# Cosformer attention and SwiGLU on one core: features of q turned whole, early loads uncast, banks by age

## The chip, the cores and the metric

The kernel runs on one core of a Trainium2 chip. The metric is device time in microseconds (us), the median of several executions. "Span" is the profiled execution's own length, some 2 us shorter than its time. "Turned" means transposed, "uncast" loaded without a change of type. TensorE multiplies, VectorE and ScalarE do elementwise work, GpSimd issues the loads that cast (the software queue), SP issues uncast loads, stores and DMA transposes (the hardware queue). The profile counts the packets of both queues on the same 16 DMA engines. Batches are numbered 0 to 7.

## The reference, cut to what matters

```python
# q, k, v: (8 batches, 8 heads, 576 positions, 64), float32
theta = np.pi / 2.0 * pos / S
phi = lambda x: np.concatenate([relu(x) * cos(theta), relu(x) * sin(theta)], axis=-1)
kv  = einsum('bhsf,bhsd->bhfd', phi(k), v)         # 128 features x 64
num = einsum('bhsf,bhfd->bhsd', phi(q), kv)
den = einsum('bhsf,bhf->bhs',  phi(q), sum of phi(k) over s) + 1e-06
x   = (num / den), heads side by side              # 4608 tokens x 512
out = (silu(x @ w_gate) * (x @ w_val)) @ w_out     # d_ff = 1536
```

## The kernel before

The 4608 tokens are nine groups of 512; a group is four tiles of 128 tokens, and a tile is two slots of 64 tokens. A group's FFN has 12 steps of 8 products and then 4 output tiles of 12 products. Attention for the next group is planned into numbered places between those steps: group g has places 16g to 16g + 15. In these traces TensorE runs its products in program order: while one waits, those behind it wait too.

For batches 2 to 7, q passes a ReLU on ScalarE, is turned by a DMA transpose, and each tile makes four products of 260 columns. They hold the cosine and the sine part apart; ScalarE and VectorE weight and add them afterwards:

```python
def qturn_dma(b, e):
    nc.sync.dma_start_transpose(out=qt_of(b)[:, e]..., in_=st[b, "q"][e * SH:(e + 1) * SH]...)

def a_half(t, j):                      # twice for each tile
    ps = take(2)
    for e in range(2):
        nc.tensor.matmul(out=ps[ms, e, 0:4 * D1], lhsT=st[b, "qt"][:, e, j, c:c + n]...,
                         rhs=kvd[b % 2][:, e, j]..., start=True, stop=True)   # 260 columns
    nc.scalar.activation(out=tmp, in_=av[:, :, 0], func=AF.Copy, scale=cst[:, c0, 0:1])
    nc.vector.scalar_tensor_tensor(out=num, in0=av[:, :, 1], scalar=cst[:, c0, 1:2], in1=tmp, ...)
```

Of the kernel before, what the change touches and what calls it, by code (L numbers as in the profile page):

```python
# [17 lines left out]
def kernel(  # L18
# [26 lines left out]
    R = 2 * T  # L45
# [3 lines left out]
    rel = ctx.enter_context(tc.tile_pool(name="rel", bufs=2))  # L49
    qtp = ctx.enter_context(tc.tile_pool(name="qtp", bufs=2))  # L50
    kvp = ctx.enter_context(tc.tile_pool(name="kvp", bufs=2))
# [11 lines left out]
    bank_at = [0]  # L63
    held = {}

    def take(n, hold=None):

        while True:
            b0 = (bank_at[0] + n - 1) // n * n % 8
            bank_at[0] = b0 + n  # L70
            if not any(b0 <= x < b0 + n for r in held.values() for x in r):
                break
        if hold is not None:
            held[hold] = range(b0, b0 + n)
        return banks[:, b0] if n == 1 else banks[:, b0:b0 + n]

# [23 lines left out]
    first = {}  # L100
    CUT = (4, 5)

    def load_first(nm, gs, cs=slice(0, NC)):
        if nm not in first:
            first[nm] = consts.tile([P, G, cs.stop, D], FP32, name=f"first_{nm}")
        nc.sync.dma_start(out=first[nm][:, gs, cs].rearrange("p g c d -> p g (c d)"),
                          in_=source(0, nm)[:, gs, cs.start * D:cs.stop * D])

    pairs = (slice(0, 2), slice(2, 4))
    for gs in pairs:  # L110
        load_first("v", gs)
    load_first("q", slice(0, G), slice(0, CUT[0]))
    pos_i = consts.tile([P, NC], mybir.dt.int32)
    nc.gpsimd.iota(pos_i, pattern=[[1, NC]], base=0, channel_multiplier=NC)
# [3 lines left out]
    for j in range(2):  # L118
        t = consts.tile([P, 8 * J * D1], BF16, name=f"kvd_{j}")
        nc.gpsimd.memset(t.bitcast(FP32), 0.0)  # L120
        kvd.append(t.rearrange("p (e j w i x) -> p e j w i x", e=2, j=J, w=2, i=2))
    load(0, "k", 2)
    load_slots(0, "q", CUT[0], NC)

# [4 lines left out]
    def idle_products(n):  # L129
        ps = take(1)  # L130
        for _ in range(n):
            nc.tensor.matmul(out=ps, lhsT=zeros, rhs=zeros.unsqueeze(1).to_broadcast([P, 4, P]), start=True, stop=True)  # L132

    idle_products(28)


    rad = math.pi / 2.0 / S
    bias = consts.tile([P, 3, 2], FP32)
    pos = consts.tile([P, NC], FP32)
    for i, step in enumerate((S, S - 1, S + NC - 1)):  # L140
        for e in range(2):
            hs = slice(e * SH, (e + 1) * SH)
            nc.vector.memset(bias[hs, i, 0:1], math.pi / 2.0 + e * rad * step)
            nc.vector.memset(bias[hs, i, 1:2], -e * rad * step)
        if i == 0:
            nc.vector.tensor_copy(out=pos, in_=pos_i)
    csk = consts.tile([P, NC, 2], FP32)
    cst = consts.tile([P, NC, 2], FP32)
    last = slice(NC - 1, NC)
    for i, cs, sl in ((0, csk, slice(0, NC)), (1, cst, slice(0, NC - 1)), (2, cst, last)):  # L150
        nc.scalar.activation(out=cs[:, sl, 0], in_=pos[:, sl], func=AF.Sin, scale=-rad, bias=bias[:, i, 0:1])
        nc.scalar.activation(out=cs[:, sl, 1], in_=pos[:, sl], func=AF.Sin, scale=rad, bias=bias[:, i, 1:2])
    tiny = consts.tile([P, 1], FP32)
    nc.scalar.activation(out=tiny, in_=bias[:, 0, 0:1], func=AF.Silu)
# [14 lines left out]
    wo_sb = consts.tile([P, FC, d_model], BF16)  # L169
# [26 lines left out]
    def relu_q(b, g):  # L196
        if g == 0:
            st[b, "q"] = rel.tile([P, J, NC, 2, D], BF16, name="r_q")
        relu_op("act", st[b, "q"][:, g // 2, :, g % 2], raws[b, "q"][:, g])

    def vmul(b, g):
        nc.vector.tensor_tensor(  # L202
            out=v2s[b % 2][:, g, :, :, 0:D],
            in0=(first if b == 0 and g < 2 else {"v": raw_of(b, "v")})["v"][:, g].unsqueeze(2).to_broadcast([P, NC, 2, D]),
            in1=tab, op=ALU.mult,
        )

    def qt_of(b):
        if (b, "qt") not in st:
            st[b, "qt"] = qtp.tile([P, 2, J, NC, SH], BF16, name="qt")  # L210
        return st[b, "qt"]

    def qturn_dma(b, e):
        nc.sync.dma_start_transpose(
            out=qt_of(b)[:, e].rearrange("p j c s -> p (j c) s"),
            in_=st[b, "q"][e * SH:(e + 1) * SH].rearrange("p j c i d -> p (j c i d)"),
        )
# [34 lines left out]

    def kv_free(b):
        held.pop(("kv", b))


    NW = 8
    qw = consts.tile([P, 2, J, NW, 2, D], BF16)
    qwT = {}

    def weight_q(c, w, eng):
        o, sc = qw[:, w, :, c], csk[:, c, w:w + 1]
        i = (first["q"] if c < CUT[0] else raw_of(0, "q"))[:, :, c].rearrange("p (j i) d -> p j i d", i=2)
        if eng == "act":
            nc.scalar.activation(out=o, in_=i, func=AF.Relu, scale=sc)
        else:
            nc.vector.tensor_scalar(out=o, in0=i, scalar1=sc, scalar2=0.0, op0=ALU.mult, op1=ALU.max)

    def turn_qw(t):
        qwT[t] = consts.tile([P, 2, 2, J, 2, SH], BF16, name=f"qwT_{t % 2}")  # L270
        for w, eng in enumerate(("act", "dve")):
            ps = take(1).bitcast(BF16).rearrange("p (y e s) -> p y e s", e=2, s=SH)
            for j in range(J):
                for c in range(2):
                    nc.tensor.transpose(out=ps[:, 2 * j + c].rearrange("p e s -> p (e s)"),
                                        in_=qw[:, w, j, 2 * t + c].rearrange("p i d -> p (i d)"), identity=ident)
            (nc.scalar.copy if eng == "act" else nc.vector.tensor_copy)(  # L277
                out=qwT[t][:, w].rearrange("p e j c s -> p (j c) e s"), in_=ps[:, 0:2 * J])

    def a_tile(t):  # L280
        ps = take(2)
        for e in range(2):
            for j in range(J):
                for w in range(2):
                    nc.tensor.matmul(  # L285
                        out=ps[:, e, 2 * j * D1:2 * (j + 1) * D1],
                        lhsT=qwT[t][:, w, e, j].rearrange("p c s -> p (c s)"),
                        rhs=kvd[0][:, e, j, w].rearrange("p i x -> p (i x)"),
                        start=(w == 0), stop=(w == 1),
                    )  # L290
        num = ps[:, :, 0:2 * J * D1].rearrange("p e (y x) -> p e y x", x=D1)
# [4 lines left out]
        nc.vector.reciprocal(out=rec, in_=den)  # L296
        x = xp.tile([P, d_model], BF16, name="x")
        nc.vector.tensor_tensor(
            out=x.rearrange("p (y e d) -> p e y d", e=2, d=D), in0=num[:, :, :, 0:D],
            in1=rec.rearrange("p (e y) o -> p e y o", e=2).to_broadcast([P, 2, 2 * J, D]), op=ALU.mult,  # L300
        )
# [46 lines left out]
    def x_turn(t, fast=False):  # L348
        x = st.pop(("x", t))
        tg, off = divmod(t, GH // 2)  # L350
        if tg not in xT:
            xT[tg] = xtp.tile([P, KC, T], BF16, name="xT")
        o = xT[tg][:, :, off * P:(off + 1) * P]
        if fast:
# [7 lines left out]

    ht = consts.tile([P, FC, R], BF16, name="ht")

    def ffn_mm(tg, fc, lo=0, hi=GH):

        n = (hi - lo) * SH
        ts = slice(lo * SH, hi * SH)
# [6 lines left out]
        for o, w in zip(ps, (wg_sb, wv_sb)):  # L375
            for kc in range(KC):
                nc.tensor.matmul(out=o, lhsT=w[:, kc, fs], rhs=xT[tg][:, kc, ts],  # L377
                                 start=(kc == 0), stop=(kc == KC - 1))
        st["f", tg, fc, lo] = ps

    def ffn_act(tg, fc, lo=0, hi=GH):
# [4 lines left out]
        r = (tg * T + lo * SH) % R  # L386
        nc.vector.tensor_tensor(out=ht[:, fc, r:r + n], in0=sg[:, 0:n], in1=ps[1], op=ALU.mult)  # L387
# [8 lines left out]
    def ffn_out(t, f0=0, f1=None):  # L396
# [4 lines left out]
        r = (t * P) % R  # L401
        for fc in range(f0, f1):
            nc.tensor.matmul(out=o_ps[t], lhsT=ht[:, fc, r:r + P], rhs=wo_sb[:, fc],  # L403
# [4 lines left out]
        held.pop(("o", t))  # L408
# [6 lines left out]
    def ffn_out_last(t):  # L415

        r = (t * P) % R
        for lo, hi in ((0, 320), (320, d_model)):
            ps = take(1)[:, 0:hi - lo]
            for fc in range(FC):  # L420
                nc.tensor.matmul(out=ps, lhsT=ht[:, fc, r:r + P], rhs=wo_sb[:, fc, lo:hi],  # L421
# [9 lines left out]
    for i in range(4):  # L431
        load_w(i)
# [32 lines left out]


    vmul(0, 0)
    vmul(0, 1)
    for g in (2, 3):
        nc.scalar.copy(out=raw_of(0, "v")[:, g], in_=first["v"][:, g])  # L470
        vmul(0, g)
    for c in range(CUT[0]):
        weight_q(c, 0, "act")
        weight_q(c, 1, "dve")
    relu_k(0, 0, 2, "dve")
    turn_qw(0)
    kv_mm(0, 0)
    idle_products(2)
    relu_k(0, 2, 4, "dve")
    turn_qw(1)  # L480
    kv_out(0, js=slice(0, 1))
    kv_mm(0, 1)
    idle_products(4)
    kv_out(0, js=slice(1, 2))
    kv_free(0)
    a_tile(0)
    a_tile(1)
    idle_products(3)
    for c in (4, 5):
        weight_q(c, 0, "act")  # L490
        weight_q(c, 1, "act")
    x_turn(0, fast=True)
    turn_qw(2)
    for c in (6, 7):
        weight_q(c, 0, "act")
        weight_q(c, 1, "dve")
    a_tile(2)
    for f in range(2):
        ffn_fc(0, f, 0, 2)
    x_turn(1, fast=True)  # L500
    turn_qw(3)
    for f in range(2):
        ffn_fc(0, f, 2, 4)
    x_turn(2, fast=True)
    a_tile(3)
# [108 lines left out]
```

## Time and profile before

| | before |
|---|---|
| time, median | 339.96 us (339.66 to 344.24); 339.81 with a fourth execution |
| span of the profiled run | 337.0 us, TensorE clock 1.00 |
| first FFN product | 18.23 us |
| group 1 starts | 61.55 us |
| a group in steady state | 34.36 or 34.82 us |

The prediction below shows the views that it rests on. One line that it passed over is from the view of the turned q tile: the times of its twelve DMA transposes from issue to landing.

```profile
DMA to landing us min/median/max: 3.7/3.9/10.2
```

### The profile page before, as it was taken

What the parts mean: (1) busy time and instruction counts of PE and PEld (TensorE: products, weight loads), DVE (VectorE), ACT (ScalarE), POOL (GpSimd) and SP (SyncE); (2) the same over time, 40 slices, a digit from 0 to 9 for tenths busy, and PEclk for the clock granted to TensorE, in tenths of its full rate; (3) what the DMA queues carried; (4) which work ended last, traced back from release to release, by engine and by line L of the source; (5) the groups of instructions that cost most, each with busy time, mean ns of one, the idle gap of its engine ahead of it and who ended that gap; (6) DMA issues with size and microseconds to landing.
All of it is one profiled execution on the core that took longest, in us unless ns stands there. A gap on an engine that the chain in (4) does not pass through costs nothing.

```text
span 337.0 us, 5960 instructions
## 1 busy us (share of the span) xinstructions
PE 325.9 (97%) x2280; PEld 167.6 (50%) x2313; DVE 189.0 (56%) x424; ACT 158.0 (47%) x311; POOL 32.4 (10%) x50
## 2 busy tenths in 40 slices
PE   8889998999999999999999999999999999999995
PEld 3578854454444444444454444544454444444443
DVE  6664756389526952695259625971478138714420
ACT  6664456778326732673257415751354135413321
POOL 9454320011002000200000000000000000000000
PEclk9999999999999999999999999999999999999999
DMA  8999999999976828492810271017301410141013
GB/s 238 198 200 200 204 207 208 252 185 186 159 150 100 147 58 168 72 168 48 160 27 17 48 153 45 16 31 143 71 17 31 104 38 16 34 109 31 0 33 93
DMA packets 57084, 36.76 MB, mean 109 GB/s; under 512 B 31328, under 2 KB 52064, under 8 KB 57056
## 3 DMA queue, kind: packets, MB, share of 16 engines
q0 software_dynamic: 20624, 18.03, 33.8%
q1 hardware_dynamic: 36272, 18.23, 25.9%
q8 instruction: 18, 0.29, 0.3%
q10 hardware_dynamic: 160, 0.13, 0.1%
q14 instruction: 10, 0.08, 0.1%
HBM read 37.75 MB, written 9.44 MB: 140 GB/s over the span
## 4 chain that ended last, share of the span: by engine, by line
PE 93%; ACT 3%; DVE 2%; issue 1%; ACTq 0%
PE banks L377 53%; PE banks L403 27%; PE banks L316 5%; PE banks L132 3%; PE banks L237 3%; ACT sg L385 1%; DVE v L202 1%; DVE ht L387 1%; PE banks L357 1%; PE banks L421 0%; PE banks L285 0%; ACT xT L358 0%; PE banks L223 0%; ACT ob L410 0%; ACT qwT L277 0%
## 5 line engine op out<-in xcount | busy, mean ns | idle before, releaser
L377 PE MATMUL banks<-xT,wg_sb 128*128 128x512 bf16 (+2 forms) x474 | 112.4, 354 | 1.8 <-ACT xT L358 1.0
L387 DVE TENSOR_TENSOR ht<-sg,banks 128x512 bf16<-128x512 bf16 (+2 forms) x122 | 76.1, 624 | 66.4 <-PE banks L377 50.9
L377 PE MATMUL banks<-xT,wv_sb 128*128 128x512 bf16 (+2 forms) x479 | 111.7, 354 | 0.2
L385 ACT ACTIVATE sg<-banks 128x512 bf16<-128x512 f32 (+2 forms) x122 | 66.9, 548 | 90.3 <-PE banks L377 89.4
L403 PE MATMUL banks<-wo_sb,ht 128*128 128x512 bf16 x410 | 93.3, 379 | 0.6 <-issue 0.2
L377 PEld LDWEIGHTS <-wv_sb 128*128 128x128 bf16 x488 | 47.3, 98 | 46.3
L377 PEld LDWEIGHTS <-wg_sb 128*128 128x128 bf16 x488 | 45.8, 98 | 37.1 <-issue 2.2
L403 PEld LDWEIGHTS <-ht 128*128 128x128 bf16 x420 | 40.7, 98 | 46.1 <-issue 0.6
L410 DVE COPY ob<-banks 128x512 f32<-128x512 f32 x17 | 11.8, 692 | 56.3 <-PE banks L403 56.2
L326 ACT ACTIVATE tmp<-banks,cst 128x260 f32<-128x260 f32 x64 | 30.5, 477 | 13.6 <-PE banks L316 12.8
L410 ACT COPY ob<-banks 128x512 f32<-128x512 f32 x18 | 10.6, 587 | 55.9 <-PE banks L403 55.9
L327 DVE SCALAR_TENSOR_TENSOR num<-banks,cst,tmp 128x260 f32<-128x260 f32 x64 | 31.0, 485 | 7.1 <-ACT tmp L326 6.7
L316 PE MATMUL banks<-kvd,qt 128*128 128x260 bf16 (+1 forms) x144 | 24.9, 277 | 0.1
L341 DVE TENSOR_TENSOR x<-num,rec 128x256 bf16<-128x256 f32 x64 | 24.4, 422 | 1.1
L202 DVE TENSOR_TENSOR v<-raw_v,tab 128x1152 bf16<-128x1152 bf16 x30 | 22.3, 752 | 0.0
L316 PEld LDWEIGHTS <-qt 128*128 128x128 bf16 (+1 forms) x144 | 11.8, 100 | 16.0 <-issue 3.4
L188 ACT ACTIVATE raw_k<-raw_k 128x576 bf16<-128x576 bf16 x24 | 16.0, 675 | 0.0
L188 ACT ACTIVATE r_q<-raw_q 128x576 bf16<-128x576 bf16 x24 | 16.0, 675 | 0.0
L93 POOL DMA_DIRECT2D raw_k<-in_k_dram x9 | 7.0, 780 | 82.1 <-issue 78.9
L237 PE MATMUL banks<-v,raw_k 64*64 64x130 bf16 x576 | 11.9, 220 | 1.1 <-ACT kvd L249 0.9
L237 PEld LDWEIGHTS <-raw_k 64*64 64x64 bf16 x576 | 9.2, 106 | 7.0 <-issue 5.6
L132 PE MATMUL banks<-zeros 128*128 128x512 bf16 x37 | 11.1, 458 | 1.0 <-DVE zeros L127 1.0
(57 smaller groups left out, 113.0 us busy)
## 6 DMA issues: line engine op xcount, KB each, us to landing
out_dram<-ob SPq DMA_DIRECT2D x70, 128.0 KB, 2.4
raw_k<-in_k_dram POOLq DMA_DIRECT2D x7, 576.0 KB, 12.5
raw_v<-in_v_dram POOLq DMA_DIRECT2D x6, 576.0 KB, 13.6
raw_q<-in_q_dram POOLq DMA_DIRECT2D x6, 576.0 KB, 15.6
wg_sb<-in_moe_w_gate_dram POOLq DMA_DIRECT2D x6, 256.0 KB, 11.3
wv_sb<-in_moe_w_val_dram POOLq DMA_DIRECT2D x6, 256.0 KB, 11.3
wo_sb<-in_moe_w_out_dram POOLq DMA_DIRECT2D x3, 512.0 KB, 13.3
first_v<-in_v_dram SPq DMA_DIRECT2D x2, 576.0 KB, 4.2
```

What stands on the lines that cost most here:

```text
L188: nc.scalar.activation(out=out, in_=in_, func=AF.Relu)
L202: nc.vector.tensor_tensor(out=v2s[b % 2][:, g, :, :, 0:D], in0=(first if b == 0 and g < 2 else {"v": raw_of(b, "v")})["v"][:, g].unsqueeze ...
L237: nc.tensor.matmul(out=ps[i * D:(i + 1) * D, e, j * 2 * D1:(j + 1) * 2 * D1], lhsT=raws[b, "k"][es, g, c], rhs=v2s[b % 2][es, g, c, :, 0:D ...
L316: nc.tensor.matmul(out=ps[ms, e, 0:4 * D1], lhsT=st[b, "qt"][:, e, j, c:c + n].rearrange("p c s -> p (c s)"), rhs=kvd[b % 2][:, e, j].rear ...
L326: nc.scalar.activation(out=tmp, in_=av[:, :, 0], func=AF.Copy, scale=cst[:, c0, 0:1])
L327: nc.vector.scalar_tensor_tensor(out=st["num", t][:, j], in0=av[:, :, 1], scalar=cst[:, c0, 1:2], in1=tmp, op0=ALU.mult, op1=ALU.add,)
L341: nc.vector.tensor_tensor(out=x[:, 4 * j * D:(4 * j + 4) * D].rearrange("p (i e d) -> p e i d", i=2, e=2), in0=num[:, hs, 0:D].rearrange(" ...
L377: nc.tensor.matmul(out=o, lhsT=w[:, kc, fs], rhs=xT[tg][:, kc, ts], start=(kc == 0), stop=(kc == KC - 1))
L385: nc.scalar.activation(out=sg[:, 0:n], in_=ps[0], func=AF.Silu)
L387: nc.vector.tensor_tensor(out=ht[:, fc, r:r + n], in0=sg[:, 0:n], in1=ps[1], op=ALU.mult)
L403: nc.tensor.matmul(out=o_ps[t], lhsT=ht[:, fc, r:r + P], rhs=wo_sb[:, fc], start=(fc == 0), stop=(fc == FC - 1))
L410: (nc.scalar.copy if t % 2 == 0 else nc.vector.tensor_copy)(out=ob, in_=ps)
```

## The change

It has three intents. The start is to be earlier: k, v and the first q come uncast through SP, and weights are held behind v. PSUM banks (the eight pieces of memory that TensorE writes its products to) are taken by age instead of in rotation. From batch 2 on, q is multiplied by cosine and sine before it is turned, so that one product of 65 columns per head is complete and the weighting after it goes. The turned q is then twice as large. Tile 9 is used three places later than before, and x of tiles 9 to 11 is turned on TensorE instead of by DMA. The core of the diff, cut:

```diff
-        relu_op("act", st[b, "q"][:, g // 2, :, g % 2], raws[b, "q"][:, g])
+        relu_op("act", o, o)
+        nc.vector.tensor_tensor(out=st[b, "q"][:, g], in0=o.unsqueeze(2).to_broadcast([P, NC, 2, D]),
+                                in1=tab, op=ALU.mult)
...
         nc.sync.dma_start_transpose(
-            out=qt_of(b)[:, e].rearrange("p j c s -> p (j c) s"),
+            out=phit[b][:, e].rearrange("p g c s -> p (g c) s"),      # twice as many columns
...
+    def a_tile2(t):
...
+        for e in range(2):
+            for g in range(G):
+                for ms, b, c, n in parts:
+                    nc.tensor.matmul(out=ps[ms, e, g * D1:(g + 1) * D1],
+                        lhsT=phit[b][:, e, g, c:c + n].rearrange("p c s -> p (c s)"),
+                        rhs=kv2s[b % 2][:, e, g // 2, g % 2], start=True, stop=True)
+        x_of(t, ps)
...
+    b0 = min(free, key=lambda b: sorted(used[b:b + n], reverse=True))
...
+    nc.gpsimd.tensor_copy(out=hold, in_=first["v"][:, 1, 0, 0:1])    # weights wait for v
+    load_w(0)
+    load_slots(0, "q", CUT[0], NC)
...
+        elif tg == 2:                                                # tiles 9 to 11
+            at((10, 11, 12)[i - 1] + SLOTS, lambda t=t: a_tile2(t))
+            at((12, 13, 14)[i - 1] + SLOTS, turn(t, True))
```

## The prediction

> **What bounds the kernel now.** I read the page's totals first, then busy time by stretch (cut at the first product of each group of 512 tokens), then TensorE's instructions in order of time.
>
> ```profile
> PE 325.9 (97%) x2280; PEld 167.6 (50%) x2313; DVE 189.0 (56%) x424; ACT 158.0 (47%) x311; POOL 32.4 (10%) x50
> ...
> 0.00:18.20 18.20, 15.46 (x161) 8.43 (x162) 12.36 (x42) 12.27 (x29) 12.39 (x23) 1.00 1.12 216
> 18.20:61.50 43.30, 40.35 (x434) 29.73 (x434) 25.99 (x66) 22.51 (x53) 13.30 (x18) 1.00 1.28 204
> 61.50:96.10 34.60, 34.34 (x230) 16.63 (x233) 23.08 (x48) 21.34 (x40) 2.24 (x3) 1.00 1.09 189
> ...
> 130.70:165.10 34.40, 34.19 (x229) 16.61 (x232) 20.51 (x44) 16.82 (x32) 2.23 (x3) 1.00 0.64 114
> ```
>
> TensorE (first pair after the stretch's length) is full in every stretch from 61.5 us on; VectorE (third) has 20.5 of 34.4 us and ScalarE (fourth) 16.8. Relieving those two buys nothing there: a stage shortens only by what TensorE no longer has to issue. Before 61.5 us, TensorE waits, so two different sums are needed. The ends of products are modelled, so I count from start to start:
>
> ```profile
> 133.33 1.03 PE L377 MATMUL banks<-xT,wv_sb 128*128 128x512 bf16 x4
> 134.28 0.72 PE L237 MATMUL banks<-v,raw_k 64*64 64x130 bf16 x36
> 134.94 1.04 PE L377 MATMUL banks<-xT,wg_sb 128*128 128x512 bf16 x3
> ...
> 140.88 0.38 PE L316 MATMUL banks<-kvd,qt 128*128 128x260 bf16 x2
> 141.10 1.03 PE L377 MATMUL banks<-xT,wg_sb 128*128 128x512 bf16 x4
> ```
>
> Four 512-column products take 4 x 0.216 us; two 260-column ones 141.10 - 140.88 = 0.22 us, 0.111 each; 36 small key-value products 0.66 us. The step 133.33 to 134.28 is 0.95, not 0.86: 0.09 us is lost whenever TensorE goes between full 128x128 and 64-wide weights, and the single starts in the trace show 0.09 at every such change.
>
> **What the Trainium skill says.** "TensorE: Matmul & The Clock Gate", section "Back-to-back issue gap", gives an isolated gap of N/2.4 + 2.5 ns for N columns, and 81 ns for a stream of weight-load-and-product pairs at N = 128. This trace agrees with the first (0.2158 us at 512, 0.111 at 260) and not with the second: its 128-column transposes, each with its own weights, start 0.0555 us apart. The same page, "Weight-path perf modes — Fast Weight Load (FWL) and DoubleRow", says that full 128-column weights load in four chunks side by side, about 32 cycles. Here two such loads of the transposes at 16.18 us start 15 ns apart, which fits; no product narrower than 128 columns on full weights is in this trace. "DMA: Bandwidth & Descriptors", section "SWDGE vs HWDGE vs iDMA", says that casting needs GpSimd's software path and that uncast loads can go by SP with less set-up. The trace agrees: SP's first loads start issuing at 0.74 us and bring data near 2 us, at some 400 GB/s; GpSimd's first issue at 2.37 brings its first packets about 6.3 us.
>
> **The change, part one: the stages from 61.5 us.** Tiles 9 to 35 (27 of 36) take the new form. Twenty-four lie in one batch. Before, each took 4 x 0.111 = 0.443 us; after, 8 products of 65 columns on full 128x128 weights. By the formula one is 65/2.4 + 2.5 = 29.6 ns; if the load of the next weights is not quite hidden it is more, and at the 55.5 ns of the 128-column pairs nothing would be gained. My estimate is 35 ns: 0.28 us a tile, gain 24 x 0.163 = 3.9 us. Three tiles (13, 22, 31) straddle two batches. Before: two bursts of four 64-wide products, 0.25 us each, and four changes of weight width at 0.094: 0.88 us. After: one burst of 16 products in pairs. A pair of 260-column ones now starts 0.135 us after the last, 0.024 over its columns, so I put a new pair at 54 ns: 8 x 0.054 + 2 x 0.094 = 0.62 us; gain 3 x 0.25 = 0.75 us. Against this, tiles 9 to 11 are now turned on TensorE instead of by DMA: 12 x 0.0555 = 0.67 us. Sum: 4.0 us off the path.
>
> Beside the path, each of the 27 tiles loses two ScalarE instructions (0.477) and two VectorE ones (0.485), and two multiplications of 0.422 become one of 0.69 from PSUM; batches 2 to 7 gain 24 VectorE multiplications of cos and sin, some 0.75 us each (the row for v at 128x1152 has 0.752). VectorE: -27 x 1.12 + 24 x 0.75 = -12 us. ScalarE: -27 x 0.954 = -26 us. Neither was binding. The turned q doubles; its DMA landed in 3.9 us before and is issued about eight slots (some 15 us) before its first use, so I expect it hidden.
>
> **Part two: the start.** This is TensorE now, with two waits that the change aims at:
>
> ```profile
> 0.99 8.61 PE L132 MATMUL banks<-zeros 128*128 128x512 bf16 x28 [0.99 <-DVE zeros L127]
> ...
> 17.75 0.64 PE L285 MATMUL banks<-kvd,qwT 128*128 128x130 bf16 x8 [0.72 <-ACT qwT L277]
> 18.23 0.38 PE L377 MATMUL banks<-xT,wg_sb 128*128 128x128 bf16 x4
> ...
> 57.69 0.38 PE L357 MATMUL banks<-ident,x 128*128 128x128 bf16 x4 [0.68 <-ACT ob L410]
> ...
> 60.47 0.38 PE L357 MATMUL banks<-ident,x 128*128 128x128 bf16 x4 [0.67 <-ACT ob L410]
> ```
>
> The first FFN product starts at 18.23 us. After the change v, k and the first q come uncast through SP in nine pieces. The load of v before (1.18 MB) released its users at 4.55 and 5.98 us, 1.43 us for each 0.59 MB. At that pace: k's first two pieces near 6.7 and 7.5 us, the first q 8.1, the other k pieces 8.9 and 9.6. The weights are held behind v, issued near 4.7 and, with GpSimd's four microseconds to first data, start near 8.7, so they take little from these. ScalarE has three casts of v (0.6 each) and then two ReLUs of k (0.67): done at 8.5. Then, by the durations of like rows: first half of key-value 0.8, eviction 0.45, VectorE's two k ReLUs 1.1 and two q multiplications 0.8 (to 11.8), the second half of key-value meanwhile to 11.8 and its eviction to 12.4, first attention tile to 12.7, its normalization to 14.1, turn and copy to 14.75. So the first FFN product moves from 18.23 to about 14.75.
>
> That is not all gain, because less is done by then: attention tiles 1 and 2 and their transposes now come later. Counting only start-to-start costs up to the first product of group 1, TensorE has 38.3 us of work after 18.23 in the old program and 39.3 after 14.75 in the new one. The old one took 43.3 us for it, 5.0 lost: 1.3 in early waits for x and its copy, about 1.5 in width changes, 1.7 in the two bank waits at 57.69 and 60.47 (transposes that got the bank which ScalarE had just begun to copy out), the rest small. The new one keeps the width changes and a little more (q's later transposes are 64 wide), takes the oldest bank and so loses the two bank waits, and has new waits early on: the weights of f 2 and 3 land near 17.2 us while TensorE gets there near 17, and each early tile waits for q, x and copies. I put its loss at 3.9. Group 1 then starts at 14.75 + 39.3 + 3.9 = 58.0 instead of 61.5: 3.5 us.
>
> **Sum.** 4.0 + 3.5 = 7.5 us, on a median of 339.96: 332.4 us; I say 332.2, a ratio of 0.977.
>
> **Rivals.** (1) The 65-column products are bound by the weight load, near 55 ns: for it, the skill's 81 ns and the fact that no narrow product on full weights is in the trace; against it, loads 15 ns apart. Part one would then give 0.1 us, and the time 336. (2) The start is limited by the weights' DMA: the same bytes come at the same 400 GB/s read, and weights that wait behind v and k can starve the FFN; the order of a and b halves also asks for f 8 near 28.3 us while its weights land near 28.2. One to three microseconds would come back: 333 to 335. (3) VectorE takes TensorE's place for some slots: in group 1 it gets four extra q multiplications in two slots (2 x 0.75 + 0.685 = 2.2 us in a 1.73 us slot) and ends some 4 us behind. Six unheld banks are three units of work, 5 us, so I expect almost no wait; at worst 2 us. In later groups eight slots hold 8 x 1.43 + 4 x 1.06 = 15.7 us of VectorE work against some 15 of TensorE, too little to fill the banks. (4) The turn of x reads four strided runs of 128 per product instead of 512 in a row; a few ns on 768 products would cost 2 us or so. Nothing in the trace says so. (5) The other way: 30 ns products, and an early start without new waits: 329.
>
> **Range and chances.** The narrow product moves the time by -1 to +4 us, the start by 2 either way. Range 328.5 to 336.3. The 2% line is 333.2, near my middle, but the errors that I can name are not all on one side of it: faster 0.62, same 0.37, slower 0.01.
>
> **What would show it.** Starts of the 65-column products 30 to 40 ns apart, with stages of about 33.7 us from group 3 on (34.4 now). First FFN product at 14 to 15.5 us, group 1 at 57 to 59. No transposes waiting for an output copy. VectorE near 177 us and ScalarE near 130 to 135. I am wrong if the narrow products start 55 ns apart, if waits for weights' DMA stand in the first 35 us, or if TensorE waits for VectorE in group 1.

## More of the kernel before

Batch 2's turn is planned at place 18 and first used in group 1 by tile 9, at place 23 (26 after the change). The loads of later batches run ahead. They have three buffers for each of k, v and q, and GpSimd issues them as soon as a buffer is free, wherever in the program they stand:

```python
for s, nm in ((p0 - 2, "k"), (p0, "v"), (p0 + 2, "q")):    # b > 3
    at(s, lambda b=b, nm=nm: load(b, nm))
```

## The result, and the profile after

The changed kernel took 351.75 us (median; 351.02 to 352.18), against 339.81 for the kernel before. The ratio is 1.0358, interval 1.0328 to 1.0387: slower. Ratios here are the mean time of one kernel's fast runs over that of the other's from the same rounds, so they are not quite the ratios of the medians quoted.

First the page of the changed kernel, its totals and the row of the granted clock in 40 equal slices; then its busy time by stretch, with the columns as in the prediction.

```profile
PE 324.5 (93%) x2484; PEld 165.6 (47%) x2484; DVE 179.3 (51%) x365; ACT 134.9 (39%) x253; POOL 31.6 (9%) x49
...
PEclk9999999998569999999999999999999999999999
```

```profile
59.60:109.50 49.90, 33.26 (x238) 15.85 (x237) 25.49 (x47) 19.52 (x35) 2.22 (x3) 0.83 1.01 137
...
143.00:176.60 33.60, 33.60 (x250) 16.07 (x248) 19.35 (x36) 13.66 (x24) 2.23 (x3) 1.00 0.81 136
```

TensorE has no more work than before (324.5 us busy), but one stretch has only 33.26 busy of 49.90 us. It is in group 1, and the clock falls there. TensorE's instructions in order of time show where; the brackets give idle time and what ended it.

```profile
79.72 1.03 PE L480 MATMUL banks<-xT,wv_sb 128*128 128x512 bf16 x4
88.55 0.40 PE L380 MATMUL banks<-kv,phit 128*128 128x65 bf16 x4 [7.80 <-DMA phit<-r_q]
97.78 0.40 PE L380 MATMUL banks<-kv,phit 128*128 128x65 bf16 x4 [8.83 <-DMA phit<-r_q]
97.99 1.90 PE L480 MATMUL banks<-xT,wg_sb 128*128 128x512 bf16 x4
99.68 1.91 PE L480 MATMUL banks<-xT,wv_sb 128*128 128x512 bf16 x4
```

The first tile of the new form stands twice: for the first half of batch 2's turned q (L380, `phit`) and for the second. From start to start, over what the products take, the waits are 7.97 and 9.05 us. The next eight FFN products start 0.43 us apart, not 0.216: the granted clock fell to 0.50 during the wait and is still there (0.50 from 85 to 101.5 us), which costs 1.67 us more. Together that is 18.7 us.

The sums by milestone, each from the starts of TensorE's products:

| us | before | after | difference |
|---|---|---|---|
| start to group 1 | 61.55 | 59.63 | -1.9 |
| group 1 | 34.37 | 53.48 | +19.1 |
| groups 2 to 6, five together | 173.19 | 168.80 | -4.4 |
| group 7 | 32.85 | 32.11 | -0.7 |
| group 8 and the end | 35.1 | 34.9 | -0.2 |
| span | 337.0 | 348.9 | +11.9 |

Why did the turn land so late? Three views of the changed kernel: SP's queue (how long the issue of the two halves took), from issue to landing, and the DMA packets between 78 and 88 us (packets, MB, share of 16 engines).

```profile
65.60 27.46 SPq L253 DMA_TRANSPOSE phit<-r_q  x2
```

```profile
DMA to landing us min/median/max: 5.9/6.1/22.9
```

```profile
q0 software_dynamic: 902, 1.01, 87.2%
q1 hardware_dynamic: 1036, 0.26, 50.3%
```

In later groups a half lands in 6.1 us; in group 1 it takes 22.9. In those 10 us the loads of later batches (software) got 902 packets through and the turn 1036, nearly one for one; from 70 to 74 us it is 572 and 572. But a load's packet is 1.1 KB and the turn's is about 0.25 KB. So the turn gets a fifth of the bytes. Sharing is not all of it: between 70 and 74 us the two queues moved 200 GB/s, between 78 and 88 us 127; why stays open. The loads beside the turn are those of batch 4 and of batch 5. GpSimd's queue shows when batch 5's begin, before and after:

```profile
74.97 0.76 POOL L93 DMA_DIRECT2D raw_k<-in_k_dram  x1 [20.28 <-issue]
```

```profile
72.33 0.74 POOL L98 DMA_DIRECT2D raw_k<-in_k_dram  x1 [17.89 <-issue]
```

These loads are not needed until two groups later. They start just after batch 2's key-value product, when a buffer comes free. Before, batch 2's turn had landed at 76.35 and 77.38 us, just as they began, and tile 9 was due at 77.3 us. Nothing in the kernel's plan had arranged that. SP's queue and tile 9 in the kernel before:

```profile
66.11 6.83 SPq L214 DMA_TRANSPOSE qt<-r_q  x2
```

```profile
77.32 0.39 PE L316 MATMUL banks<-kvd,qt 128*128 128x260 bf16 x2
```

### The profile page after: what moved, and what is told of

Same layout as the page of the kernel before. It is cut to its first block, busy times and chain, and to the rows that moved or that the text cites. A ratio compares the mean times of both kernels' runs of the same rounds, so it can differ in the third digit from the quotient of the medians.

```text
span 348.9 us, 6209 instructions
## 1 busy us (share of the span) xinstructions
PE 324.5 (93%) x2484; PEld 165.6 (47%) x2484; DVE 179.3 (51%) x365; ACT 134.9 (39%) x253; POOL 31.6 (9%) x49
## 4 chain that ended last, share of the span: by engine, by line
PE 83%; DMA 14%; POOL 1%; issue 0%; ACT 0%; ACTq 0%; SPq 0%; DVE 0%; DVEq 0%
PE banks L480 50%; PE banks L507 26%; DMA phit<-r_q 6%; DMA wv_sb<-in_moe_w_val_dram 4%; DMA wg_sb<-in_moe_w_gate_dram 3%; PE banks L276 3%; PE banks L380 2%; DMA wo_sb<-in_v_dram 1%; PE banks L415 1%; PE banks L526 0%; PE banks L462 0%; PE banks L262 0%; POOL hold L541 0%; POOL wg_sb L201 0%; ACT ob L529 0%
## 5 line engine op out<-in xcount | busy, mean ns | idle before, releaser
L480 PE MATMUL banks<-xT,wv_sb 128*128 128x512 bf16 (+2 forms) x496 | 114.6, 354 | 1.4 <-DMA wv_sb<-in_moe_w_val_dram 1.4
L480 PE MATMUL banks<-xT,wg_sb 128*128 128x512 bf16 (+2 forms) x496 | 114.8, 354 | 0.1
L490 DVE TENSOR_TENSOR ht<-sg,banks 128x512 bf16<-128x512 bf16 (+2 forms) x124 | 76.4, 617 | 60.4 <-PE banks L480 51.3
L380 PE MATMUL banks<-kv,phit 128*128 128x65 bf16 (+1 forms) x240 | 12.0, 198 | 16.6 <-DMA phit<-r_q 16.6
L230 DVE TENSOR_TENSOR r_q<-raw_q,tab 128x1152 bf16<-128x1152 bf16 x24 | 17.9, 751 | 18.7 <-DMA phit<-r_q 18.7
L380 PEld LDWEIGHTS <-phit 128*128 128x128 bf16 (+1 forms) x240 | 10.7, 103 | 24.1 <-DMA phit<-r_q 17.3
L398 DVE TENSOR_TENSOR x<-banks,rec 128x512 bf16<-128x512 f32 (+1 forms) x32 | 21.5, 674 | 1.1
L213 ACT ACTIVATE raw_q<-raw_q 128x576 bf16<-128x576 bf16 x24 | 16.0, 674 | 0.0
L98 POOL DMA_DIRECT2D raw_k<-in_k_dram x7 | 5.2, 742 | 98.3 <-issue 63.3
L148 PE MATMUL banks<-zeros 128*128 128x64 bf16 (+1 forms) x64 | 9.4, 311 | 1.0 <-DVE zeros L143 1.0
L276 PE MATMUL banks<-v,raw_k 64*64 64x130 bf16 x504 | 10.2, 220 | 0.0
L463 ACT COPY xT<-banks 128x512 bf16<-128x512 bf16 x10 | 5.9, 588 | 3.9 <-PE banks L462 3.9
```

The costliest lines, as they stand in the source:

```text
L148: nc.tensor.matmul(out=ps, lhsT=zeros, rhs=zeros[:, 0:cols].unsqueeze(1).to_broadcast([P, 4, cols]), start=True, stop=True)
L213: nc.scalar.activation(out=out, in_=in_, func=AF.Relu)
L230: nc.vector.tensor_tensor(out=st[b, "q"][:, g], in0=o.unsqueeze(2).to_broadcast([P, NC, 2, D]), in1=tab, op=ALU.mult)
L276: nc.tensor.matmul(out=ps[i * D:(i + 1) * D, e, j * 2 * D1:(j + 1) * 2 * D1], lhsT=raws[b, "k"][es, g, c], rhs=v2s[b % 2][es, g, c, :, 0:D ...
L380: nc.tensor.matmul(out=ps[ms, e, g * D1:(g + 1) * D1], lhsT=phit[b][:, e, g, c:c + n].rearrange("p c s -> p (c s)"), rhs=kv2s[b % 2][:, e, ...
L398: nc.vector.tensor_tensor(out=xv[:, :, ys], in0=num[:, :, ys, 0:D], in1=rv[:, :, ys].to_broadcast([P, 2, ys.stop - ys.start, D]), op=ALU.mult)
```

## The experiments

Theory A: batch 2's turn shares the DMA engines packet for packet with loads that nobody needs yet, and ends only when they end. Rival B: the doubled turn is slow by itself. Rival C: the features come late from VectorE. Rival D: something in the new start other than loads holds the turn up. All results were correct. Waits in this section are from start to start, over what the products take.

| run | us | ratio (95% interval) |
|---|---|---|
| after | 351.75 | 1.0358 (1.0328 to 1.0387) |
| e1_loads_wait | 333.03 | 0.9797 (0.9762 to 0.9832) |
| e2_late_loads_wait | 333.97 | 0.9821 (0.9787 to 0.9854) |
| e3_before_turn_twice | 354.87 | 1.0390 (1.0313 to 1.0468) |
| e4_old_products | 351.61 | 1.0256 (1.0160 to 1.0352) |
| e5_before_banks | 340.40 | 1.0018 (0.9983 to 1.0054) |
| e6_paced | 332.25 | 0.9776 (0.9746 to 0.9805) |
| e7_paced_x_by_dma | 334.49 | 0.9844 (0.9813 to 0.9876) |
| e8_old_products_paced | 338.10 | 0.9942 (0.9904 to 0.9980) |
| e9_before_twice_paced | 341.26 | 1.0047 (1.0026 to 1.0069) |
| e10_before_paced | 339.24 | 0.9986 (0.9968 to 1.0004) |
| e11_paced_weights_first | 333.74 | 0.9810 (0.9790 to 0.9831) |
| e12_paced_f8_later | 332.81 | 0.9791 (0.9770 to 0.9813) |

**The loads of batches 4 and later wait for batch 2's turn.** A small read makes GpSimd wait; no wait is taken away.

```diff
+                if b == 4:
+                    at(p0 - 2, lambda: nc.gpsimd.tensor_copy(out=hold2, in_=phit[2][:, :, 0, 0, 0]))
                 for s, nm in ((p0 - 2, "k"), (p0, "v"), (p0 + 2, "q")):
```

> Changed kernel, but GpSimd reads two numbers of the turned q of batch 2 before it issues the loads of batches 4 and later, so those loads cannot share the DMA engines with that turn. Theory A (the turn, twice as large, is interleaved packet by packet with loads that nobody needs yet, and so ends only when they end): the turn lands by about 76 to 78 us instead of 88.5 and 97.7, the waits of 8.0 and 9.0 us and the 1.7 us of slow clock after them go, 332 to 335 us. Rival B (the doubled turn is slow by itself, in its issue on SP): still lands near 88 and 98 us, 351 us or more. Rival C (the features come late from VectorE): the issue of the turn moves or nothing changes, 350 us.

Measured: 333.03 us. SP's queue and TensorE at tile 9:

```profile
65.24 9.09 SPq L253 DMA_TRANSPOSE phit<-r_q  x2
```

```profile
80.22 0.42 PE L380 MATMUL banks<-kv,phit 128*128 128x65 bf16 x8
```

The same two transposes, of the same size and issued within 0.4 us of the same time, take 9.09 us to issue instead of 27.46. They land at 72.8 and 76.3 us, and tile 9 does not wait. The clock stays at 1.00. So the turn is not slow by itself (B), nor late from VectorE (C). A wait of 1.2 us remained at tile 13: batch 3's turn now met the loads of batches 5 and 6.

**Only the loads of batch 5 and later wait** (the same edit with `b == 5`).

> As the run before, but only the loads of batch 5 and later wait for the turn of batch 2; those of batch 4 still run beside it until about 79 us. Theory A: the two halves of the turn land near 80 and 84 us, TensorE waits 2 to 5 us at tile 9, 334 to 338 us. Rival B: 351 us. If the loads of batch 4 alone are to blame, about 350 us.

Measured: 333.97 us. The turn landed at 79.8 and 81.9 us, and TensorE waited 1.1 us at tile 9, less than I had expected. TensorE at the second half:

```profile
81.92 0.30 PE L380 MATMUL banks<-kv,phit 128*128 128x65 bf16 x4 [0.90 <-DMA phit<-r_q]
```

Batch 5's loads were what cost nearly all of the wait. Batch 4's alone are almost harmless to the time, but not to the turn: its first half took 14.1 us to land beside them and 7.6 in the run before. They use up the room.

**The kernel before, with each turn done twice,** the first time into memory no longer used.

```diff
     def qturn_dma(b, e):
+        nc.sync.dma_start_transpose(
+            out=spare.rearrange("p (y s) -> p y s", s=SH), in_=st[b, "q"][e * SH:(e + 1) * SH]...)
```

> Kernel before, with one thing of the change added: every DMA turn of q is done twice, the first time into memory that is no longer used; same products, same VectorE work, right result. Theory A: the second half of batch 2's turn lands near 88 us instead of 77.4, tile 9 is due at 77.5 us, so TensorE waits about 10 us there and 346 to 354 us come out; later batches land in some 6 us and cost nothing. Rival C (features late from VectorE, or the new form of the products): 340 us, as the kernel before.

Measured: 354.87 us. TensorE at tile 9:

```profile
77.73 0.27 PE L320 MATMUL banks<-kvd,qt 128*128 128x260 bf16 x1
90.20 0.40 PE L320 MATMUL banks<-kvd,qt 128*128 128x260 bf16 x1 [12.19 <-DMA qt<-r_q]
```

The doubled turn alone, put into the kernel before, brings the whole slowdown, with the old products and no new VectorE work. The second half landed at 90.15 us. The wait also cost some of the clock and 0.9 us at the start of group 2.

**The changed kernel with the old products and the old, smaller turn** in all batches: what is left are its start and its banks.

```diff
-        nc.vector.tensor_tensor(out=st[b, "q"][:, g], in0=o.unsqueeze(2)..., in1=tab, op=ALU.mult)
+        relu_op("act", st[b, "q"][:, g // 2, :, g % 2], raws[b, "q"][:, g])
...
-            at(s, lambda t=t: a_tile2(t), turn(t))
+        at(s, a_(t, 0))
+        at(s + 1, a_(t, 1), turn(t))
```

> Changed kernel with its new start and its banks by age, but the old products of 260 columns and the old, half as large turn of q in all batches. Theory A: no wait of over 3 us at tile 9 (the old turn landed at 77.4 us just as it was due; here TensorE gets there some 2 us earlier), groups of 34.4 us again, group 1 at 59.6 us: 337.5 to 340.5 us. If the start or the banks were what costs the time, it would stay at 345 us or more.

Measured: 351.61 us, so my number was wrong by 12. Two of its four runs counted as slow (over 1.5% above its fastest) and the two fast ones took 346.42 and 351.23; even the fastest shows the loss. The profile is of a 351.99 us run. TensorE at tile 9:

```profile
79.44 0.40 PE L413 MATMUL banks<-kvd,phit 128*128 128x260 bf16 x1 [3.44 <-DMA phit<-r_q]
87.62 0.40 PE L413 MATMUL banks<-kvd,phit 128*128 128x260 bf16 x1 [7.78 <-DMA phit<-r_q]
```

The old turn, not doubled, is late too: 79.4 and 87.6 us instead of 76.4 and 77.4. The new start moved three things. Batch 4's last load landed at 79.1 instead of 75.8 us, at the end of a software queue whose first packets start at 9.7 instead of 6.5 us. Batch 5's loads were issued at 72.8 instead of 75.0. And tile 9 was due at 75.8 instead of 77.3. So the new start (with the banks by age) and the doubled turn each suffice to push the turn into batch 5's loads. Their costs do not add: what matters is falling over the edge. Whether loads were the cause here was open until run e8.

**Banks by age alone, in the kernel before** (the new `take`, with its two helpers).

> Kernel before with only the choice of banks by age added. The two waits of 0.84 us at 57.69 and 60.47 us (transposes of x that got the bank which ScalarE was copying out) go: 338 us. Theory A warns that being earlier can cost: the loads of batch 5 go out as soon as batch 2's key-value product is evicted, so they come about 1.7 us earlier while the loads of batch 4 end at the same time; if they then catch the second half of batch 2's turn, a wait of several us at tile 9 and up to 350 us come out instead.

Measured: 340.40 us, the same as before. The two waits of 0.84 us for an output copy are gone and group 1 starts at 60.30 us, 1.3 us earlier. But tile 9 then waits 2.2 us, since the second half of the turn landed at 78.4 us. The gain is given back at the next wait, the milder of the two outcomes foreseen.

**The changed kernel, paced:** every batch's loads from 4 on wait for the turn of the batch two before.

```diff
+                at(p0 - 2, lambda b=b: nc.gpsimd.tensor_copy(out=hold2, in_=phit[b - 2][:, :, 0, 0, 0]))
```

> Changed kernel with every batch's loads from batch 4 on held until the turn of the batch two before has landed. Theory A: no wait for a turn anywhere (the 1.2 us at tile 13 that remained when only batch 2's turn was protected goes too), 331.5 to 332.5 us. If the held loads come too late for their batch, waits for raw k, v or q appear instead and the time is over 333 us.

Measured: 332.25 us, the best version; its interval (0.9746 to 0.9805) lies below 1. By stretch:

```profile
59.50:94.00 34.50, 34.40 (x256) 16.86 (x256) 25.41 (x47) 20.62 (x38) 2.41 (x4) 1.00 0.99 162
...
127.80:161.50 33.70, 33.65 (x249) 16.08 (x249) 19.35 (x36) 13.66 (x24) 2.41 (x4) 1.00 0.87 137
```

TensorE is full in both, and no turn takes over 7.5 us to land. The edit undoes nothing of the change and takes 19.5 us off it.

**Paced, with x of tiles 9 to 11 turned by DMA** instead of on TensorE (`turn(t)` for `turn(t, True)`, two places earlier).

> As the paced kernel, and x of tiles 9 to 11 turned by DMA again instead of on TensorE. Twelve transposes of 0.0555 us go from TensorE: 0.7 us less than the paced kernel, about 331.2 us, if the DMA is done before group 2 starts; if it is not, a wait at the start of group 2 and 332 us or more.

Measured: 334.49 us, a miss. TensorE at the start of group 2:

```profile
96.17 1.04 PE L480 MATMUL banks<-xT,wg_sb 128*128 128x512 bf16 x4 [2.29 <-DMA xT<-x]
```

x's turns, issued at 83.7 to 93.7 us, landed at 91.1 to 96.1: beside batch 4's loads and behind batch 3's turn. The 0.7 us on TensorE that I had booked as a cost of the change buys more than it costs.

**Old products and old turn, paced** (the edit of e6 on e4).

> New start and banks by age with the old products and the old turn, and the loads paced in the same way. Theory A: the waits of 3.6 and 8.1 us at tile 9, which this kernel had without pacing, go; groups of 34.4 us; group 1 starts near 59.5 us: 337 to 339 us. The difference to the paced kernel is then what the 65-column products give by themselves: 5 us. Rival D (the old turn is held up by something in the new start other than the loads, such as its single buffer for r_q): 345 us or more.

Measured: 338.10 us. The waits at tile 9 are gone (the turn landed at 70.1 and 72.2 us), so D falls and loads were the cause in e4 too. TensorE at tile 9:

```profile
77.09 0.38 PE L413 MATMUL banks<-kvd,phit 128*128 128x260 bf16 x2
```

Its runs fall into two sets: 336.77 to 337.34 us at a clock of 0.998 to 1.000, and 338.85 to 339.24 at 0.992 to 0.995. The profile is of one of the latter; the clock drops in it between 20 and 24 us (0.57), after two waits for weights. By the medians the start and the banks give 339.37 - 338.10 = 1.3 us (2.3 in the first set) and the 65-column products 338.10 - 332.25 = 5.9 us (4.8 against the first set's 337.06).

**The kernel before, turns doubled, paced** (e3 with the edit of e6).

> Kernel before with every turn of q done twice (354.9 us without pacing), and the loads from batch 4 on held until the turn of the batch two before has landed. Theory A (the loads beside it, not the size of the turn, are what cost): the wait of 12.4 us at tile 9 goes, 339 to 342 us. If the size alone were enough, a wait of several us stays and 345 us or more.

Measured: 341.26 us, 13.6 less than without pacing, with no wait over 0.2 us at tile 9:

```profile
79.14 0.57 PE L320 MATMUL banks<-kvd,qt 128*128 128x260 bf16 x2
```

Size without loads beside it is nearly harmless. A wait of 0.8 us for x at group 2 belongs to what is left over the kernel before; the rest is open, as the profiled run had a later start.

**The kernel before, paced.**

> Kernel before with the loads paced and nothing else. In it the turn of batch 2 already landed just when tile 9 was due, so pacing has nothing to win: 339 to 340 us, as before. A gain of over 1 us would mean that part of what the paced changed kernel wins over the kernel before is the pacing and not the change.

Measured: 339.24 us, ratio 0.9986: nothing. What e6 wins over the kernel before is the change, not the pacing alone.

**Paced, weights first:** the second pair of weights before the rest of q, and q's later early turns after the products.

```diff
     load_w(0)
+    load_w(1)
     load_slots(0, "q", CUT[0], NC)
```

> The paced changed kernel with its early waits for weights taken up: the second pair of weights is loaded before the rest of q, q's third and fourth early turns come after the products that these weights allow, and f 8 comes one step later. The paced kernel waited 0.6 and 1.1 us at f 2 and 0.9 us at f 8; most of that goes: 330 to 331.5 us. If the rest of q then comes too late, a wait of about 1 us takes their place and it stays at 332 us.

Measured: 333.74 us, a miss. The waits for weights went, but each tile then waited for its x or its q (0.9, 0.8, 0.6 and 0.5 us). The profiled run, 335.87 us, also had the first k late, so it does not stand for the median.

**Paced, f 8 one step later.**

> The paced changed kernel (332.25 us) with one thing altered: f 8 of the first half group comes one step later, after its weights have landed. The wait of 0.9 us there goes and nothing else changes: about 331.4 us, ratio to the kernel before about 0.975. If it stays at 332.3 us, something else sets the pace of the first group.

Measured: 332.81 us. In the profiled run (331.35 us) the wait at f 8 is gone, as expected. But four of six runs took 332.8 to 333.2 us at a clock of 0.994 or 0.995, the others 331.35 and 331.54 at 0.999 and 1.000. Its gain in time is thus not shown; this run and e6 were also on different chips, and their intervals overlap. What makes the clock fall in some executions of this start stays open.

## Why the prediction was wrong

The failed step is this one: "The turned q doubles; its DMA landed in 3.9 us before and is issued about eight slots (some 15 us) before its first use, so I expect it hidden." The 3.9 us was the median of twelve. The turn that the plan has least room for, batch 2's, had taken 10.2 us, and had landed at 77.38 us for a tile due at 77.3: no room at all. I should have looked up that one transfer. The room that I named is real: in the new plan the first half is issued at 65.60 us and tile 9 is due at 80.6. What failed is the cost. The old turn's halves together had needed 11.3 us (66.11 to 77.38); doubling that gives an estimate of 22.6 us, already more than 15. They took 32.1 (65.60 to 97.73). The runs put in its place: the turn took 22.9 us beside loads (351.75 us) and about 7.5 without them (333.03 us). Of the rivals, none had it: I looked for the DMA wait in the weights, and for VectorE in group 1, and gave "slower" a chance of 0.01.

The Trainium skill has a mechanism that fits. "DMA: Bandwidth & Descriptors", section "Queues, rings and completion order", says that each DMA engine goes round its queues a packet at a time. The 572 and 572 packets of 70 to 74 us agree, if the profile's packets are the ones that the page means, which no run here shows. That this is what shares out the bytes is argued from those counts; that the loads beside the turn are the cause is shown by e1, e6, e8 and e9.

Point by point:

- **The 65-column products.** Right. In the profiled run eight of them start 0.0323 us apart on average (estimate 0.035, rival 0.055). Steady groups take 33.62 or 33.85 us; I had said about 33.7.
- **Tiles across two batches.** Right in kind, better in size. Sixteen products of 64-wide weights, with one change of width at each end:

```profile
126.11 1.03 PE L480 MATMUL banks<-xT,wv_sb 128*128 128x512 bf16 x4
127.07 0.45 PE L380 MATMUL banks<-kv,phit 128*64 128x65 bf16 x16
127.45 1.04 PE L480 MATMUL banks<-xT,wg_sb 128*128 128x512 bf16 x4
```

From 126.97 (four products of 0.216 after 126.11) to 127.45 is 0.48 us, against 0.62 estimated.
- **Part one as a sum.** 4.0 us expected; groups 2 to 8 of the changed kernel are 5.3 us shorter (4.4 + 0.7 + 0.2), and e6 against e8 says 5.9 by the medians, 4.8 by e8's runs at full clock. So it was 1.3 us too small.
- **Waits for an output copy.** Right: gone, here and in e5.
- **The start.** Right in direction, 1.6 us too good: group 1 at 59.63 instead of 58.0. The first FFN product came at 15.55 (14.75 expected): k's four pieces landed at 8.3, 9.2, 10.7 and 11.8 us instead of 6.7, 7.5, 8.9 and 9.6. And waits for weights took more than I allowed:

```profile
19.49 0.40 PE L480 MATMUL banks<-xT,wv_sb 128*128 128x128 bf16 x4 [0.91 <-DMA wv_sb<-in_moe_w_val_dram]
```

From one start to the next that is 1.08 us at f 2, and 0.61 more near 31 us: rival 2, at its low end.
- **VectorE in group 1 (rival 3).** No wait of TensorE for it (34.40 of 34.50 us busy there in e6). VectorE came to 179.3 us (177 expected), ScalarE to 134.9 (130 to 135).
- **x read in strided runs (rival 4).** No effect: the products start 0.216 us apart as before.
- **Two readings.** GpSimd's first packets in the kernel before start at 6.5 us, not 6.3, and the 128-column transposes start 0.056 us apart, not 0.0555. Nothing hangs on either.

With its loads paced the change took 332.25 us, and 332.2 was predicted. So close a hit is luck: by the profiles part one brought 1.3 us more than I said and the start 1.6 us less, and the two errors cancel. It does not excuse the failed step, which was worth 19.5 us.

## What to carry to other kernels

Before a transfer is made larger, look up that transfer's own landing and the moment of its first use, not the median of its kind: one that arrives just in time is a cliff, and small shifts of other work can push it over. Here prefetch that ran as far ahead as its buffers allowed held up an urgent transfer of small packets. A small read that held it back cost nothing in the kernel before (339.24 against 339.52 us) and was worth 19.5 us in the changed one, more than the change itself wins.

## What the Trainium skill lacked or had wrong

- "DMA: Bandwidth & Descriptors": it gives the turn-taking between queues by packet, but not what this does to a DMA transpose beside loads. Here a half of the turn took 22.9 us instead of 6.1, with 1036 packets of some 0.25 KB against 902 of 1.1 KB in 10 us.
- The same page, "Specifications", gives about 1 us to the first byte on GpSimd's path. In the kernel before, the first issue began at 2.37 us and the first packets started at 6.5 us, 4.1 later. That holds for the first DMA of the kernel alone, a case that the page does not set apart: at 103.24 us, with the queue empty, packets started 1.46 us after the issue began.
- "TensorE: Matmul & The Clock Gate", "Back-to-back issue gap": 81 ns for pairs of weight load and product at N = 128 was not seen; the runs show 56 ns, and 32.3 ns at 65 columns on full weights, near the page's own N/2.4 + 2.5.
- "TensorEngine Tiling (Array Packing)", "Key Properties", says that a change of tiling mode drains TensorE, without a number. The runs show 0.093 to 0.100 us at each change.
